# Last block's inverse by TensorE transposes, tokens stationary in the expert layer, rows of h on VectorE, a new order

## The chip, the cores and the metric

The kernel runs on one core of a Trainium2 chip, in one launch. The metric is device time in microseconds (us). Engines are called TensorE (PE), VectorE (DVE), ScalarE (ACT), GpSimd (POOL) and SyncE (SP, which issues nearly all transfers). Tensors on the chip lie on 128 partitions; TensorE writes to PSUM, and VectorE or ScalarE must copy results out of it.

## The reference, cut to what matters

Token count S is 2048, channels D are 640, inputs are bfloat16. Mixer A is a long convolution over tokens (an FFT of length 4096 in the reference), mixer B sends the 8 tokens with the largest router score through a gated expert layer and adds the result to their rows.

```python
def A(q, k, v, shift_k, ssm_k, ssm_D):
    kv = causal_conv4(k, shift_k) * v              # per channel, 4 taps
    y = irfft(rfft(kv, 2*S) * rfft(ssm_k, 2*S))[:S]  # per channel, over tokens
    return q * (y + kv * ssm_D)
def B(x, w_r, w_gate, w_up, w_down):
    r = x @ w_r; idx = argsort(-r)[:8]; xs = x[idx]
    y = (silu(xs @ w_gate) * (xs @ w_up)) @ w_down     # 640 -> 1728 -> 640
    return x.at[idx].add(y * sigmoid(r[idx]))
sa, ca, ga, sb, cb, gb = (silu(c) @ w_mod).reshape(6, 640)
x = A_q
x = x + ga * A(layernorm(x) * (1 + ca) + sa, A_k, A_v, ...)
x = x + gb * B(layernorm(x) * (1 + cb) + sb, ...)
```

Here h is layernorm(x)*(1+ca)+sa times ga, the factor on y; it is needed for every token and channel.

## The kernel before, in words

The 640 channels are five blocks of 128 (b = 0 to 4), the tokens 16 tiles of 128. A block goes through: G and X (first transform stage of the filter and of kv, line 435), BG and BX (second stage, 501, copied out into HX), P (the product in the frequency domain on VectorE, 513 to 519), BT (the first half of the inverse, 538, copied out of PSUM as U), UW and LU (U written to DRAM, 546, and read back in another layout as uA, 556: this exchanges channels with one of the token digits between partitions), AT (the second half, 575, which leaves tokens on the partition and is multiplied by h, 83 to 89), AA (added onto x, 586). Then R (594 on: transposes of x by TensorE, 644, copied out as xT, and the router's and the mean's dot products, 654) and GR (the squares of every row by small products, 596) run per block; when all five are summed, T makes the second layernorm's factors and picks the 8 tokens (860 to 901). The tail runs N (normalised rows, 839 and 842), BS and BL (x plus a row, 614 to 638), F (two VectorE passes over pairs of token tiles and the store to the output, 850 to 853), and between them the gather of the 8 rows (917), the gate and up products (935), the product hT (970) and the down product (978). The last step adds 40 pieces of 128 channels onto the output with an indirect transfer (988), after all stores have landed.

Lines 71 and 73 are the common copy out of PSUM: on VectorE where an entry of the order carries a star, else on ScalarE. t_H (line 787) makes h: a tensor_scalar for each of 16 token tiles (on GpSimd under a star), and two VectorE passes of 4 tiles by 640 (792).

The order is written out by hand: the string ORDER names task steps, and a loop runs them one after the other; each engine executes its own instructions in that order, and SP issues transfers one after the other, each behind the waits of those ahead. SLOTS gives the buffer of each allocation. In the functions below, tails of long helpers that the diff leaves alone are as in the program.

Of the kernel before, what the change touches and what calls it, by code (L numbers as in the profile page):

```python
# [22 lines left out]
NFC = 14  # L23
FFP = NFC * P
# [51 lines left out]
def _kernel_body(ctx, tc, A_q, A_k, A_v, A_shift_k, A_ssm_k, A_ssm_D,  # L76
# [75 lines left out]
    v_d = A_v.flatten_outer_dims().rearrange("(m p) d -> p m d", p=P)  # L152
    xq_d = A_q.flatten_outer_dims().rearrange("(m p) d -> p m d", p=P)
# [78 lines left out]
    keys = const.tile([P, M], F32, name="keys")  # L232
    mask8 = const.tile([NB * NSEL, NSEL], F32, name="mask8")
# [92 lines left out]
    def t_TC():  # L326
# [197 lines left out]
    def t_BT(b):  # L524
        hx = HXs[b]
        Ud = Uds[b] = dram.tile([P, M, 256], BF, name="Ud%d" % b)
        for hk in range(2):
            U = ring.tile([P, 8, 256], BF, name="U", tag="K", bufs=5)
            for kk in range(2):
# [10 lines left out]
                evac(U[:, 4 * kk:4 * kk + 4, :], ps[:])  # L540
                Us[b, hk] = U
# [24 lines left out]
    def t_AT(b):  # L566
        h = h_["h"]
        c0 = b * P
        for hb in range(2):
# [11 lines left out]
            yield  # L581

# [58 lines left out]
    def t_R(b):  # L641
        pt = ps_tile([P, M, P], BF)
        for m in range(M):
            nc.tensor.transpose(pt[:, m, :], xq[:, m, b * P:(b + 1) * P], ident[:])
        xTs[b] = ring.tile([P, M, P], BF, name="xT", tag="K", bufs=5)[:]
        if b == NB - 1:
            V.tensor_copy(out=xTs[b][:, 0:8, :], in_=pt[:, 0:8, :])
            nc.scalar.copy(out=xTs[b][:, 8:M, :], in_=pt[:, 8:M, :])
        else:
            evac(xTs[b], pt[:])  # L650
        yield
# [42 lines left out]
    def rows(i, scale, gate, shift):  # L694
# [4 lines left out]
        V.tensor_tensor(out=cg[:, NB:2 * NB], in0=modc[:, shift, :], in1=modc[:, gate, :], op=ALU.mult)  # L699
        pt = ps_tile([2 * NB, P], BF)  # L700
# [96 lines left out]
    def t_WG():  # L797

        w_sb = W["g"] = ring.tile([P, NB, FFP], BF, name="wg", tag="A", bufs=2)
        nc.gpsimd.memset(w_sb[:, :, FF:FFP], 0.0)  # L800
# [3 lines left out]
        w_sb = W["u"] = ring.tile([P, NB, FFP], BF, name="wu", tag="A", bufs=2)  # L804
        nc.gpsimd.memset(w_sb[:, :, FF:FFP], 0.0)
# [50 lines left out]
    def t_T():  # L856
# [220 lines left out]
```

## Time and profile before

| what | us |
|---|---|
| median of 3 runs | 178.72 (177.79 to 180.08) |
| profiled execution, its own time | 177.24 |
| its span, first to last instruction | 175.2 |
| VectorE busy / TensorE busy / ScalarE busy | 150.5 / 143.5 / 138.7 |

The median is 1.48 us above the profiled execution, and that 2.04 us above its span. A busy share over the whole span hides that the first 118 us and the last 57 us are bound differently; the rows below are therefore taken by stretch.

### The profile page before, as it was taken

The numbers are of one execution on the slowest core, as the hardware profiler recorded it, in microseconds if no ns is written. First come the engines' busy times: TensorE is split into PE (matmuls) and PEld (weight loads), VectorE is DVE, ScalarE is ACT, GpSimd is POOL, SyncE is SP. The second block draws the span as 40 slices with busy tenths as digits, with TensorE's granted clock in tenths as the row PEclk, the third lists the DMA queues.
The fourth block names the chain that finished last, engine by engine and source line by source line (L and its number), as shares of the span: only waits on it lengthen the run. The fifth ranks groups of instructions, "written<-read, shape, count | busy, mean of one in ns | idle before, by whom it ended". The sixth has DMA issues, their size and how long they took to land.

```text
span 175.2 us, 5348 instructions
## 1 busy us (share of the span) xinstructions
PE 143.5 (82%) x2296; PEld 118.2 (67%) x2299; DVE 150.5 (86%) x277; ACT 138.7 (79%) x156; POOL 57.1 (33%) x80
## 2 busy tenths in 40 slices
PE   7898997999899999889796999999679492699310
PEld 2487976887778867768685878988579440647300
DVE  7799999999999989999999999999946487799710
ACT  3769998999999999679987999999924249989200
POOL 8106299999000035909993001000000040000003
PEclk9999999999999999999999999999978879569655
DMA  6999999999995499478075782869792900495420
GB/s 135 207 230 226 260 269 259 207 282 322 283 310 122 99 321 247 172 199 280 23 223 239 205 261 120 281 207 308 230 343 34 332 13 2 105 340 185 146 77 2
DMA packets 54550, 35.51 MB, mean 203 GB/s; under 512 B 32057, under 2 KB 51966, under 8 KB 54526
## 3 DMA queue, kind: packets, MB, share of 16 engines
q1 hardware_dynamic: 54320, 35.15, 71.2%
q8 instruction: 18, 0.29, 0.8%
q0 software_dynamic: 80, 0.01, 0.2%
q14 instruction: 6, 0.05, 0.1%
q10 hardware_dynamic: 126, 0.01, 0.0%
HBM read 24.67 MB, written 7.87 MB: 186 GB/s over the span
## 4 chain that ended last, share of the span: by engine, by line
DVE 46%; PE 21%; DMA 13%; issue 7%; ACT 5%; POOL 3%; SPq 3%; POOLq 1%; DVEq 0%; ACTq 0%
DVE st L775 5%; DVE HX L514 5%; DVE T L513 5%; DMA Ud<-U 4%; DVE h L792 4%; DVE HX L71 4%; DVE kv L89 4%; DMA uA<-Ud 3%; PE ps L538 3%; DMA vN<-in_A_v_dram 3%; DMA out_dram<-IT 3%; SPq L163 2%; PE ps L473 2%; DVE A L71 2%; PE ps L435 2%
## 5 line engine op out<-in xcount | busy, mean ns | idle before, releaser
L73 ACT CAST A<-ps 128x1024 bf16<-128x1024 f32 x28 | 27.7, 1043 | 2.5 <-PE ps L435 2.5
L73 ACT CAST HX<-ps 128x1024 bf16<-128x1024 f32 x26 | 26.2, 1056 | 0.3
L787 POOL TENSOR_SCALAR h<-xq,rs,nm 128x640 bf16<-128x640 bf16 x12 | 19.9, 1671 | 2.1 <-PE p L435 2.1
L473 PEld LDWEIGHTS <-kT 128*128 128x128 bf16 x320 | 18.4, 98 | 3.0 <-issue 1.4
L501 PE MATMUL ps<-A,FX 128*128 128x256 bf16 x132 | 18.3, 273 | 1.8 <-DVE U L71 1.2
L538 PE MATMUL ps<-IT,HX 128*128 128x256 bf16 x112 | 18.0, 273 | 0.6 <-DVE HX L519 0.3
L501 PEld LDWEIGHTS <-FX 128*128 128x128 bf16 x160 | 14.7, 97 | 5.3 <-issue 3.3
L538 PEld LDWEIGHTS <-HX 128*128 128x128 bf16 x160 | 15.2, 98 | 3.4 <-issue 1.2
L73 ACT CAST U<-ps 128x1024 bf16<-128x1024 f32 x13 | 13.3, 1037 | 1.0 <-PE ps L538 0.7
L514 DVE TENSOR_TENSOR HX<-HX 128x2048 bf16<-128x2048 bf16 x10 | 13.7, 1374 | 0.3
L775 DVE BATCH_NORM_STATS2 st<-xq 128x6 f32<-128x320 bf16 x32 | 13.6, 478 | 0.0
L375 POOL TENSOR_SCALAR dg<-ident,shk_f 128x128 bf16<-128x128 bf16 x12 | 9.1, 772 | 13.0 <-DVE trig L408 8.8
L792 DVE TENSOR_TENSOR h<-h,modv 128x2560 bf16<-128x2560 bf16 x8 | 12.5, 1566 | 0.0
L575 PE MATMUL ps<-RAT,uA 128*128 128x128 bf16 x144 | 10.1, 232 | 2.9 <-DMA uA<-Ud 2.9
L73 ACT CAST base<-ps 128x1024 bf16<-128x1024 f32 x8 | 7.8, 1014 | 5.7 <-PE ps L620 5.7
L575 PEld LDWEIGHTS <-uA 128*128 128x128 bf16 x160 | 10.0, 104 | 3.3 <-DMA uA<-Ud 3.1
L513 DVE TENSOR_TENSOR T<-HX 128x2048 bf16<-128x2048 bf16 x10 | 12.1, 1214 | 0.0
L473 PE MATMUL p<-dg,kT 128*128 128x128 bf16 x160 | 10.1, 219 | 1.5 <-DVE dg L375 0.7
L538 PE MATMUL ps<-IT,T 128*128 128x256 bf16 x56 | 10.7, 273 | 0.0
L435 PEld LDWEIGHTS <-gF 128*64 128x64 bf16 x160 | 8.1, 109 | 3.7 <-issue 3.3
L988 POOL DMA_INDIRECT out_dram<-delta,idx x1 | 1.7, 1677 | 26.7 <-issue 26.7
L435 PEld LDWEIGHTS <-xA 128*64 128x64 bf16 x160 | 8.2, 109 | 3.2 <-issue 2.8
(263 smaller groups left out, 369.8 us busy)
## 6 DMA issues: line engine op xcount, KB each, us to landing
Ud<-U SPq DMA_DIRECT2D x10, 512.0 KB, 3.7
uA<-Ud SPq DMA_DIRECT2D x10, 512.0 KB, 5.3
early<-in_w_mod_dram SPq DMA_DIRECT2D x6, 800.0 KB, 7.6
gA<-in_A_ssm_k_dram SPq DMA_DIRECT2D x5, 512.0 KB, 6.6
vN<-in_A_v_dram SPq DMA_DIRECT2D x5, 512.0 KB, 5.5
xq<-in_A_q_dram SPq DMA_DIRECT2D x4, 640.0 KB, 6.4
wg<-in_B_w_gate_dram SPq DMA_DIRECT2D x5, 432.0 KB, 6.5
wu<-in_B_w_up_dram SPq DMA_DIRECT2D x5, 432.0 KB, 7.2
```

Source lines behind the costliest of these rows:

```text
L71: self.nc.vector.tensor_copy(out=out, in_=in_)
L73: self.nc.scalar.copy(out=out, in_=in_)
L435: nc.tensor.matmul(ps[o, bb // 2, :, (bb % 2) * 8:(bb % 2) * 8 + 8].rearrange("p (k c) e -> p k c e", c=2), lhsT=src[:, 4 * g4 + bb, o], r ...
L473: nc.tensor.matmul(ps[:, i, :], lhsT=kT[:, n0 - j:n0 - j + P], rhs=diags[b][:, j, :], start=(j == 0), stop=(j == 3))
L501: nc.tensor.matmul(ps[:, i], lhsT=FX[:, k2, :], rhs=A[:, 2 * k2:2 * k2 + 2, u, :], start=True, stop=True)
L513: V.tensor_tensor(out=T2[:], in0=X, in1=Hi, op=ALU.mult)
L514: V.tensor_tensor(out=X, in0=X, in1=Hr, op=ALU.mult)
L538: nc.tensor.matmul(ps[:, i, :], lhsT=a, rhs=IT[:, k2, d:d + 2, :].rearrange("p a b -> p (a b)"), start=(n == 0), stop=(n == len(terms) - 1))
L575: nc.tensor.matmul(o, lhsT=uA[:, bb, cs * P:(cs + 1) * P], rhs=RAT[:, cs, :].rearrange("p (m e) -> p m e", e=8), start=(cs == 0), stop=(cs ...
L775: V.bn_stats(out=st1[:, m, hf, :], in_=xq[:, m, hf * 320:hf * 320 + 320])
L787: (nc.gpsimd if evac.vector else V).tensor_scalar(out=h[:, m, :], in0=xq[:, m, :], scalar1=rs1[:, m:m + 1], scalar2=nm1[:, m:m + 1], op0=A ...
L792: V.tensor_tensor(out=hq, in0=hq, in1=row[:, None, :].to_broadcast([P, 4, D]), op=op)
```

## The change

The changed program does this. Block 4 no longer goes through DRAM: its BT copies are written in a strided layout, 16 blocks of 128x128 per half are transposed by TensorE (t_XT), copied out by VectorE and ScalarE, multiplied with the same table RAT with the data stationary, and give the inverse with channels on the partition. For that layout q's last block is read with a transposing transfer (t_LQT), h's last block is transposed by TensorE and scaled on the way out (t_HT), the sum is the xT that R and GR need, and t_RB transposes it back into x. In the expert layer the 8 tokens (padded to 32) are the stationary operand, in four column groups of 32 that take different tokens or columns; the gather's four partial sums are added by a product with S8. Hidden size 1728 is cut as 16 x 108, not 13.5 x 128. The rows of h are all on VectorE, and the two passes skip the last block. ORDER and SLOTS are new throughout; the strings are not shown beyond a line.

```diff
-UW4 AT1* AA0 BT4 LU3 BT4 AA0 AA1 AT2 LU3 GB:2 UW4 WG COL LU4 AA1 AT2* AA2:2 R0 AT3*:2 GR R1 LU4 AA3 R2 AA3 AT4 R0 GR
+BX4 AA1 P4 AT2* GR AA2 BG4 AA2 R1 BT4 UW3 P4 BT4 LU3 LQT GR P4 HT R2* AT3* R1 LU3 BT4 AA3 BT4 AT3 WG R2 AA3 XT BS* GR
 def t_BT(b):
-                evac(U[:, 4 * kk:4 * kk + 4, :], ps[:])
+                if b < NB - 1:
+                    evac(U[:, 4 * kk:4 * kk + 4, :], ps[:])
+                else:
+                    k0 = 8 * hk + 4 * kk
+                    for hf in range(2):
+                        o = Us[b][hf][:, :, :, k0:k0 + 4]
+                        i_ = ps[:].rearrange("p k (c j) -> p c j k", c=2)[:, :, 64 * hf:64 * hf + 64, :]
+                        ...
+def t_LQT():
+    lT["q"] = ring.tile([P, M, P], BF, name="qT4", tag="V")
+    nc.sync.dma_start_transpose(out=lT["q"][:]..., in_=q_d[:, (NB - 1) * P:D])
+def t_HT():
+    for m in range(M):
+        nc.tensor.transpose(pt[:, m, :], h_["h"][:, m, (NB - 1) * P:D], ident[:])
+    nc.scalar.activation(out=lT["h"][:], in_=pt[:], func=ACT.Identity, scale=hcol[:, 0:1], bias=hcol[:, 1:2])
+def t_XT():
+    for hf in range(2):
+        for i in range(M):
+            nc.tensor.transpose(pt[:, i, :], U[:, i * P:(i + 1) * P], ident[:])
+        V.tensor_copy(out=Vs[hf][:, 0:8, :], in_=pt[:, 0:8, :])
+        nc.scalar.copy(out=Vs[hf][:, 8:M, :], in_=pt[:, 8:M, :])
+    for hf in range(2):
+        for i in range(8):
+            for cs in range(2):
+                nc.tensor.matmul(ps[:, i, :], lhsT=Vs[hf][:, 8 * cs + i, :], rhs=RAT[:, cs, :], start=(cs == 0), stop=(cs == 1))
+        times(chunk(tT[:, :, hs]), ps[:]..., chunk(lT["h"][:, :, hs]))
+        V.tensor_tensor(out=xT[:, :, hs], in0=lT["q"][:, :, hs], in1=tT[:, :, hs], op=ALU.add)
 def t_H():
-                (nc.gpsimd if evac.vector else V).tensor_scalar(out=h[:, m, :], in0=xq[:, m, :], ...)
-            hq = h[:, 4 * m4:4 * m4 + 4, :]
+                V.tensor_scalar(out=h[:, m, :], in0=xq[:, m, :], ...)
+            hq = h[:, 4 * m4:4 * m4 + 4, 0:w]      # w = 512
 # gather, gate and up, down
-                nc.tensor.matmul(pxs[:, b, :] ..., lhsT=xq[:, m, b * P:(b + 1) * P], rhs=onehot[:, m, :], ...)
+                    nc.tensor.matmul(pX[32 * j:32 * j + 32, f0:f1], lhsT=oh32[:, m, :], rhs=xq[:, m, f0:f1], ...,
+                                     tile_position=(0, 32 * j))
+        V.tensor_copy(out=xg[:, 0:256], in_=pX[:, 0:256])
+        nc.scalar.copy(out=xg[:, 256:D], in_=pX[:, 256:D])
+            nc.tensor.matmul(px[:, NSEL * b:NSEL * b + NSEL], lhsT=xg[:, b * P:(b + 1) * P], rhs=S8[:], ...)
-                    nc.tensor.matmul(pp[:, fc - f0, :], lhsT=w_sb[:, b, fc * P:(fc + 1) * P], rhs=xsT[:, b, :], ...)
+                    nc.tensor.matmul(pp[32 * j:32 * j + 32, :], lhsT=xsT[:, b, :], rhs=w_sb[:, b, FQ * j:FQ * j + FQ], ...,
+                                     tile_position=(0, 32 * j))                       # FQ = 432
+        V.tensor_tensor(out=hh[:], in0=gs[:], in1=pgu[1][:], op=ALU.mult)
+            nc.tensor.transpose(pT[0:FC, i, :], hh[:, FC * i:FC * i + FC], ident[:])   # 4 of them
+        V.tensor_copy(out=hT[0:FC], in_=pT[0:FC]...)
+                for t in range(f0, f0 + 8):                                            # 80 products, 70 before
+                    nc.tensor.matmul(pyT[:, b, :], lhsT=W["d"][0:FC, t, b * P:(b + 1) * P], rhs=hT[0:FC, t % 4, t // 4, :], ...)
```

The order on the queues moves at three places that matter below. First SP, the transfers around the last round trip, before (Ud is the DRAM copy of U, the number tells blocks apart: 1889 is block 3, 2036 block 4; wu and wd are expert weights):

```order
L546 DMA Ud_1889<-U 128x2048
L546 DMA Ud_2036<-U 128x2048
L556 DMA uA<-Ud_1889 128x8x256 x2
L546 DMA Ud_2036<-U 128x2048
L807 DMA wu<-in_B_w_up_dram 128x1728
L556 DMA uA<-Ud_2036 128x8x256 x2
L807 DMA wu<-in_B_w_up_dram 128x1728 x3
```

and now (1846 is block 3, the last that goes through DRAM):

```order
L570 DMA Ud_1846<-U 128x2048 x2
L580 DMA uA<-Ud_1846 128x8x256
L609 DMA_TRANSPOSE qT_2353<-in_A_q_dram 128x2048
L580 DMA uA<-Ud_1846 128x8x256
L881 DMA wg<-in_B_w_gate_dram 128x1728 x2
L885 DMA wu<-in_B_w_up_dram 128x1728 x2
```

Block 4's four transfers are gone, and the transposing read of q stands between the two halves of block 3's read.

Second VectorE, from the last product P of block 4 (519) on, before:

```order
L519 TENSOR_TENSOR HX<-HX,T_2010 128x8x128
L87 TENSOR_TENSOR t<-t,h 128x1024 x4
L586 TENSOR_TENSOR xq<-xq,t 128x16x64 x3
L89 TENSOR_TENSOR t<-ps,h 128x1024
L719 TENSOR_SCALAR mc<-modc 128x5
```

and now (527 is the same product, 561 the copy of block 4's last U):

```order
L527 TENSOR_TENSOR HX<-HX,T_2337 128x8x128
L71 COPY xT<-ps 128x2048
L87 TENSOR_TENSOR t<-t,h 128x1024
L734 TENSOR_TENSOR rsum<-rsum,pq 128x48
L665 TENSOR_TENSOR xq<-xq,t 128x16x64
L561 CAST U<-ps 128x128x4
L89 TENSOR_TENSOR t<-ps,h 128x1024
L734 TENSOR_TENSOR rsum<-rsum,pq 128x48
L665 TENSOR_TENSOR xq<-xq,t 128x16x64
L634 COPY V<-ps 128x1024
```

The multiplications and additions of blocks 0 to 2 (and xT copies) now stand ahead of block 4's last U, not behind it.

Third VectorE at the very end, before:

```order
L850 TENSOR_TENSOR IT<-IT,modv 128x1280
L970 TENSOR_TENSOR hT<-gs,ps 128x56 x2
L852 TENSOR_TENSOR IT<-IT,base 128x1280
L981 COPY yT<-pg 128x40
L986 SCALAR_TENSOR_TENSOR delta<-pq,sig,gb_119 40x128
```

and now:

```order
L1041 TENSOR_TENSOR gs<-gs,pg 128x432
L1046 COPY hT<-ps 108x128
L928 TENSOR_TENSOR IT<-IT,base 128x1280
L926 TENSOR_TENSOR IT<-IT,modv 128x1280
L928 TENSOR_TENSOR IT<-IT,base 128x1280
L926 TENSOR_TENSOR IT<-IT,modv 128x1280
L1056 COPY yT<-pg 128x40
L928 TENSOR_TENSOR IT<-IT,base 128x1280
L1061 SCALAR_TENSOR_TENSOR delta<-pq,sig,gb_119 40x128
```

The copy of the down product's result (yT) now stands ahead of the last add of F (928).

## Rows read from the trace of the kernel before

**Rows 1.** Page: span, and each engine's busy time with its share.
```profile
span 175.2 us, 5348 instructions
PE 143.5 (82%) x2296; PEld 118.2 (67%) x2299; DVE 150.5 (86%) x277; ACT 138.7 (79%) x156; POOL 57.1 (33%) x80
```

**Rows 2.** Stretches: length; busy PE, PEld, DVE, ACT, POOL; granted clock, DMA share, GB/s.
```profile
0.00:118.40 118.40, 108.56 (x1405) 90.32 (x1406) 113.45 (x180) 106.20 (x120) 53.14 (x71) 1.00 0.83 222
118.40:142.10 23.70, 18.03 (x574) 16.45 (x573) 16.35 (x39) 12.37 (x10) 1.41 (x6) 0.87 0.72 232
145.40:165.50 20.10, 11.96 (x263) 8.76 (x265) 17.43 (x42) 17.25 (x24) 0.00 (x0) 0.77 0.49 166
165.50:175.20 9.70, 1.73 (x51) 1.35 (x48) 0.57 (x3) 0.00 (x0) 1.68 (x1) 0.50 0.16 44
...
164.80:167.50 2.70, 2.39 (x71) 2.05 (x71) 0.93 (x2) 0.00 (x0) 0.00 (x0) 0.50 0.68 238
```

**Rows 3.** Chain of waits (start, us, what): block 4's round trip, and the end.
```profile
118.42 4.07 DMA Ud<-U
122.57 5.62 DMA uA<-Ud
...
165.56 4.50 DMA out_dram<-IT
```

**Rows 4.** Timeline of VectorE and GpSimd (start, us): h, with and without GpSimd beside it.
```profile
69.69 1.78 DVE L514 TENSOR_TENSOR HX<-HX 128x2048 bf16<-128x2048 bf16 x1
71.40 3.04 DVE L787 TENSOR_SCALAR h<-xq,rs,nm 128x640 bf16<-128x640 bf16 x4
78.82 14.73 POOL L787 TENSOR_SCALAR h<-xq,rs,nm 128x640 bf16<-128x640 bf16 x8
93.00 1.62 DVE L514 TENSOR_TENSOR HX<-HX 128x2048 bf16<-128x2048 bf16 x1
...
104.03 1.23 DVE L514 TENSOR_TENSOR HX<-HX 128x2048 bf16<-128x2048 bf16 x1
145.41 0.45 DVE L839 TENSOR_SCALAR xn<-xq,sn 128x640 bf16<-128x640 bf16 x1
```

**Rows 5.** Groups by line: xcount | busy us, mean ns of one | idle before.
```profile
L792 DVE TENSOR_TENSOR h<-h,modv 128x2560 bf16<-128x2560 bf16 x8 | 12.5, 1566 | 0.0
L586 DVE TENSOR_TENSOR xq<-xq,t 128x1024 bf16<-128x1024 bf16 x10 | 6.5, 686 | 0.0
L89 DVE TENSOR_TENSOR t<-ps,h 128x1024 bf16<-128x1024 f32 x3 | 3.7, 1223 | 3.9 <-PE ps L575 3.9
L647 DVE COPY xT<-ps 128x1024 bf16<-128x1024 bf16 x1 | 0.7, 691 | 0.4 <-PE ps L644 0.4
L648 ACT COPY xT<-ps 128x1024 bf16<-128x1024 bf16 x1 | 1.0, 1013 | 1.2 <-DVE xT L647 1.2
```

**Rows 6.** Timeline of TensorE matmuls (start, us to the end of the last).
```profile
118.74 1.07 PE L575 MATMUL ps<-RAT,uA 128*128 128x128 bf16 x16
128.24 1.31 PE L575 MATMUL ps<-RAT,uA 128*128 128x128 bf16 x16 [2.90 <-DMA uA<-Ud]
129.89 0.70 PE L596 MATMUL pg<-xT 128*32 128x32 bf16 x64
130.52 1.89 PE L575 MATMUL ps<-RAT,uA 128*128 128x128 bf16 x16
164.82 2.01 PE L978 MATMUL pg<-hT,wd 128*128 128x8 bf16 x70 [3.01 <-DVE hT L970]
```

**Rows 7.** Timeline of SP's queue (start, us that the issue held it).
```profile
31.23 0.52 SPq L167 DMA_DIRECT2D vN<-in_A_v_dram  x1
59.37 8.13 SPq L163 DMA_TRANSPOSE kT<-in_A_k_dram  x1
```

**Rows 8.** Timeline of VectorE in the tail, with the idle time before a row.
```profile
152.54 0.20 DVE L922 TENSOR_TENSOR xa<-pq,mc 128x40 f32<-128x40 f32 x1 [1.11 <-PE pq L917]
160.24 0.83 DVE L852 TENSOR_TENSOR IT<-IT,base 128x1280 bf16<-128x1280 bf16 x1
```

More of the change, by code (lines that the diff above doesn't have):

```diff
@@ L583, in t_AA, with t_RB @@
+    def t_RB():
+        for hf in range(2):
+            ms = slice(8 * hf, 8 * hf + 8)
+            pt = ps_tile([P, 8, P], BF)
+            for i in range(8):
+                nc.tensor.transpose(pt[:, i, :], xTs[NB - 1][:, 8 * hf + i, :], ident[:])
+            evac(xq[:, ms, (NB - 1) * P:D], pt[:])
+            yield
+    lT = {}
     def t_AA(b):
@@ L641, in t_R @@
     def t_R(b):
[L642 to L649, printed above, removed]
+        if b < NB - 1:
+            pt = ps_tile([P, M, P], BF)
+            for m in range(M):
+                nc.tensor.transpose(pt[:, m, :], xq[:, m, b * P:(b + 1) * P], ident[:])
+            xTs[b] = ring.tile([P, M, P], BF, name="xT", tag="K", bufs=5)[:]
             evac(xTs[b], pt[:])
-        yield
+            yield
         pr = small_ps([P, M, 3])
@@ L699, in rows @@
         V.tensor_tensor(out=cg[:, NB:2 * NB], in0=modc[:, shift, :], in1=modc[:, gate, :], op=ALU.mult)
+        if i == 0:
+            for a in range(2):
+                V.tensor_copy(out=hcol[:, a:a + 1], in_=cg[:, NB * a + NB - 1:NB * a + NB])
         pt = ps_tile([2 * NB, P], BF)
@@ L899, in t_T @@
         V.max(out=t8[:], in_=cand.bitcast(F32))
-        onehot = tail()[:, 1280:1408].rearrange("p (m s) -> p m s", m=M)
+        onehot = oh32[:, :, 0:NSEL]
         V.tensor_tensor(out=onehot, in0=keys[:, :, None].to_broadcast([P, M, NSEL]),
@@ L928, in t_T @@
-        V.tensor_tensor(out=xsT[:, 3:5, :], in0=xsf[:, 3:5, :], in1=xb[:, 3:5, :], op=ALU.add)
+        V.tensor_tensor(out=xsf[:], in0=px[:, 0:NB * NSEL].rearrange("p (b s) -> p b s", b=NB), in1=xa[:], op=ALU.mult)
+        V.tensor_tensor(out=xsT[:, :, 0:NSEL], in0=xsf[:], in1=xb[:], op=ALU.add)
         yield
-        def proj(pp, w_sb, f0, f1):
+        pgu = small_ps([P, FQ]), other_ps([P, FQ])
+        gs = small.tile([P, FQ], BF, name="gs")
+        for pp, w_sb in zip(pgu, (W["g"], W["u"])):
@@ L945, in t_T @@
-        for i in range(2):
-            proj(pup[:, i, 0:HF * NSEL].rearrange("p (f s) -> p f s", s=NSEL), W["u"], i * HF, i * HF + HF)
+                for j in range(4):
+                    nc.tensor.matmul(pp[32 * j:32 * j + 32, :], lhsT=xsT[:, b, :], rhs=w_sb[:, b, FQ * j:FQ * j + FQ],
+                                     start=(b == 0), stop=(b == NB - 1), tile_position=(0, 32 * j), skip_group_check=True)
+        nc.scalar.activation(out=gs[:], in_=pgu[0][:], func=ACT.Silu)
         yield
```

157 lines of the change are left out of this document (91 added, 66 removed).

## The prediction, made before the changed kernel was run

> **What bounds the kernel now.** I read the page first: VectorE is busy longest, but at 86% [rows 1], so the share has to be split. The stretches do that [rows 2]. Up to 118.4 us VectorE works 113.45 us, TensorE has its full clock, and whatever VectorE is given there lengthens the stretch. From 118.4 to 142.1 VectorE works only 16.35 of 23.70 us and ScalarE 12.37: nobody is full, so something else sets the end. The chain of waits says what [rows 3]: after block 4's last copy the data goes to DRAM (118.42) and back (122.57), and TensorE starts the second half of its inverse at 128.24 [rows 6], 9.8 us later. Everything behind it (R, GR, the second layernorm) waits for that block. From 145.4 to 165.5 VectorE is near its limit again, 17.43 of 20.10 us, with F's sixteen passes as the body. The last 9.7 us are the last store (4.50 us), the scatter and its landing, and contain almost no work.
>
> So the end is a sum of four: t0 (block 4's last U copy, 118.4), 23.7 to the start of T, 3.3 for T, 20.1 for the tail, 9.7. Durations on VectorE I count from start to start, 0.07 to 0.09 below a row's length (the product of 69.69 lasts 1.78, the next operation starts at 71.40 [rows 4]; F's pass is 0.83 long [rows 8] and counts 0.75).
>
> **Up to t0: what VectorE is given and spared.** Idle time there I leave as it is, 5.0 us.
> - Rows of h: twelve go from GpSimd to VectorE. The four already there took 3.04 us, 0.76 each, while GpSimd ran the same operation; the same shape and operation took 0.45 alone (145.41) [rows 4]. 12 x 0.42 = +5.0. With the crowded price it would be 9.1.
> - The two passes over h are 512 instead of 640 wide: 8 x 1.566 / 5 = -2.5 [rows 5].
> - Crowding ends: between 69.69 and 93.00 twelve VectorE operations that read SBUF ran longer than the same form elsewhere, the product of 2048 elements 1.78 and 1.62 against 1.23 [rows 4]. The excesses add up to 4.9 us, and no row of h is left on GpSimd: -4.9.
> - Moved ahead of t0 from behind it: three products with PSUM (1.13), six additions (0.60), two copies xT of 2048 elements (twice L647's 0.69, less overlap, 1.3), some eighteen small ones (1.9 in all) [rows 5]: 3.4 + 3.6 + 2.6 + 1.9 = +11.5. This work was in the half-empty stretch; it now sits in the full one, and that is the price of the change.
> - Copies out of PSUM given to ScalarE: four of HX less, three of A more, U's a half instead of a whole, one of modv and half a kv product less, net -3.0. Small things (diagonals to GpSimd, one negation from it): +0.5.
>
> Together +6.6, t0 = 125.0. ScalarE takes the extra copies and half of the moved xT, TensorE about 9 us of moved products; both had 10 to 12 us free in the 118.4 [rows 2], and the new stretch is 6.6 longer.
>
> **From t0 to T.** Before t0, AT of blocks 0 to 2, their R and two of five GR are done. Behind it VectorE has 9.8 us of work, and the chain runs: the last product and addition of block 3 and the copy V (1.1 + 0.6 + 0.7, with TensorE's 16 transposes beside them; ScalarE's half 1.0 [rows 5]), ready at t0 + 3.1. Sixteen products 1.07 [rows 6], 4.2; R's transposes of block 3 and the second sixteen, 6.2; product and addition with q 1.8, 8.0. Then R's small products (0.5), GR (0.70 [rows 6]), two passes over the squares (half L89's length each) and small ones: t0 + 10.9. T starts at 135.9, 6.2 earlier. The strided copies of U and the product with a strided h have no row; the same element counts bound them from below, twice that (0.6 more for each of four that wait) from above; I take the former since kv's products permute too and cost no more than plain ones.
>
> **The transposing read.** A transposing issue holds SP 8.13 us at worst, a plain one 0.52 [rows 7]. Behind q's stands the second half of block 3's read. Block 3's U is copied some 19 us before t0 (an estimate: ScalarE's copies in between, about 1 us each, as L648 [rows 5]), its write lands 4 later, the issue ends at t0 - 7 at worst, and the read needs 5.6 [rows 3]: t0 - 1, just in time for its products at t0. I count nothing, with no cover to spare. [...]
>
> **The tail.** VectorE gets an addition of 1024 elements (0.6), two normalised rows that ScalarE had (0.85), the gather's copy (0.35), a wider product and copy for hT (0.6 more), loses two small operations (-0.35): about +2.0 with rounding. ScalarE loses as much, so it does not bind. The wait of 1.11 us at the gather [rows 8] stays at 0 to 1.5: 80 small products go, 16 groups of four streams of 512 or 128 columns come, then two copies and five products. Two waits are new: hT (transposes in between, 0.5) and yT, where the last F pass now stands behind the down products. Those are 80 small ones; 70 took 2.01 at granted clock 0.50 [rows 2, 6], so the low clock doesn't hurt them: 2.3, with four streams of 512 columns ahead, against four F passes (3.0) as cover, 0.4 to 1.2 left. The tail had 2.7 us of idle time [rows 2]; I let old and new waits cancel: +2.0, between +0.5 and +4.5.
>
> Gate and up are 40 streams of 432 columns in four column groups. No row shows that; with four side by side (64 products of 32 columns took 0.70, 11 ns each [rows 6], less than one such column run) it is 10 x 0.2 = 2.0, one after another 8. I take 2.0, and 3.6 at the low clock, against 140 small products, 3.8 to 4.0 at the price above. [...]
>
> **Sum.** 175.2 - 6.2 + 2.0 = 171.0 for the span, 173.0 with the 2.04 us around it, against 177.24 for the profiled execution. The median of the runs stands 1.48 higher, so 174.5.
>
> **Rivals.**
> [...]
> 2. *Better filled.* VectorE's 5.0 us of idle time before t0 falls to 3 and the tail costs +0.5: span 167.5, median 171.
> 3. *The moved products wait in front of block 4 (slower).* TensorE executes in order, and AT of blocks 1 to 3 now stands ahead of block 4's BT. Where their uA has not landed, all of block 4 waits, as it did 9.8 us for its own before. One such wait of 2.9 us for each of three blocks (the wait before 128.24 [rows 6]) makes t0 133.7: span 179.7, median 183.2. Below one such wait it decides nothing; it takes two to lose the gain. Against: the writes are issued well ahead in the new queue. For: one SP queue carries them, and q's transposing read and the weights are in it.
> 4. *The round trip wasn't what held the end*, since VectorE is the bound anyway and only its order changed: then only the balance counts, +2.0 in the tail, -2.4 of spared work: within 2%.
>
> **Chances.** The forecast 0.40, rival 2 0.11, rival 1 with 4 0.31, rival 3 0.18. A measurement of this kernel tells about 2% from no change (175.1 to 182.3). The forecast is just beyond that edge, and a part of it, about 0.06, falls inside, as some of rival 1 falls short of it: faster 0.50, same 0.33, slower 0.17. The range reaches from rival 2 to the near end of rival 3: 170.5 to 181.5; the likeliest case alone is 172.5 to 176.5 by its unknown waits.
>
> **What would show it.** Right: no write or read of block 4; the last U copy near 125 and T near 136; rows of h at 0.4 to 0.5 each and the product of 2048 elements at 1.23 throughout; gate and up in 2 to 4 us; the last F pass 20 to 24 us behind T's end. Wrong: h's rows still at 0.8; TensorE waiting for uA ahead of block 4's BT; a granted clock of 0.5 between t0 and T; a VectorE wait of over 2 us at yT or at the gather. If t0 is beyond 129, the step on filling VectorE failed; if T is more than 12.5 behind t0, the step on the new chain.

## The result, and the profile after

| | median us (runs) | ratio to the kernel before, 95% interval |
|---|---|---|
| before, with one run more than above | 178.29 (177.79 to 180.08) | |
| changed | 172.37 (170.36 to 172.72) | 0.9627, 0.9525 to 0.9729 |

3.7% faster. The forecast was 174.5 with a range of 170.5 to 181.5. The profiled execution took 172.72 with a span of 170.9; the sum had said 173.0 and 171.0. That it is so close is luck: the tail came out 1.3 us longer than in the sum, t0 and the stage behind it together 1.1 longer, the end 2.3 and T 0.2 shorter. The two largest, tail and end, both come from the way in which TensorE's instructions arrive; most of this text is about them. Executions fall into two states, of which the ratios compare the faster one alone, while the medians and the profiled executions of a_trip, a_hpool and b_pad include the slower.

The page of the changed kernel, its head and the instruction queue of TensorE, to be read beside [rows 1]:

```profile
span 170.9 us, 5177 instructions
PE 143.9 (84%) x2214; PEld 114.7 (67%) x2214; DVE 151.5 (89%) x293; ACT 137.7 (81%) x157; POOL 38.6 (23%) x71
q8 instruction: 17, 0.28, 0.7%
```

Stretches, columns as in [rows 2]: up to block 4's last copy of U (t0), on to the start of T (to 137.0), the tail, the end.

```profile
0.00:125.60 125.60, 119.33 (x1693) 98.56 (x1693) 119.57 (x217) 113.17 (x128) 35.75 (x65) 1.00 0.87 220
125.60:137.00 11.40, 8.44 (x325) 7.75 (x322) 10.02 (x18) 4.47 (x4) 0.98 (x4) 1.00 0.73 193
140.10:163.50 23.40, 16.17 (x203) 8.39 (x202) 19.14 (x46) 20.03 (x25) 0.00 (x0) 0.79 0.36 126
163.50:170.90 7.40, 0.00 (x0) 0.00 (x0) 0.27 (x2) 0.00 (x0) 1.68 (x1) 0.50 0.16 46
```

So t0 is 125.6 (118.4 before), the new stage 11.4 (23.7), T 3.1 (3.3), the tail 23.4 (20.1), the end 7.4 (9.7). VectorE's timeline: four rows of h, the last copy of U, the first step of T (its last, 959, ends at 140.06), and what comes behind it.

```profile
79.02 1.51 DVE L867 TENSOR_SCALAR h<-xq,rs,nm 128x640 bf16<-128x640 bf16 x4
124.98 0.68 DVE L561 CAST U<-ps 128x512 bf16<-128x512 f32 x1
136.95 0.17 DVE L936 SCALAR_TENSOR_TENSOR n2v<-ssq,msq 128x16 f32<-128x16 f32 x1
142.89 0.69 DVE L708 TENSOR_TENSOR base<-xq,modv 128x1024 bf16<-128x1024 bf16 x1 [2.83 <-ACT xq L73]
```

Right behind T VectorE waits 2.83 us for a copy of ScalarE, and ScalarE waits 8.73 us, until 141.84, for TensorE. TensorE's timeline says why; the two rows at 152.12 and 153.05 are the gate and up products in their new form.

```profile
133.17 0.55 PE L730 MATMUL pq<-wcol,xT 128*128 128x3 bf16 x16 [1.12 <-ACT xT L73]
133.65 0.66 PE L675 MATMUL pg<-xT 128*32 128x32 bf16 x64
134.28 0.54 PE L730 MATMUL pq<-wcol,xT 128*128 128x3 bf16 x16
134.75 0.66 PE L675 MATMUL pg<-xT 128*32 128x32 bf16 x64
135.35 0.56 PE L656 MATMUL ps<-ident,xT 128*128 128x128 bf16 x7
141.54 0.27 PE L656 MATMUL ps<-ident,xT 128*128 128x128 bf16 x1 [5.63 <-issue]
...
152.12 1.10 PE L1017 MATMUL pq<-wg,xsT 128*32 128x432 bf16 x20 [0.64 <-DVE xsT L1008]
153.05 1.09 PE L1017 MATMUL pg<-wu,xsT 128*32 128x432 bf16 x20
```

TensorE stops for 5.63 us after seven of eight equal transposes, whose operands are all there. "issue" means that it waited for nothing that the profile knows. The DMA view offers a candidate: queue q8, of kind "instruction". Its 17 packets are 0.28 MB, 16 KB each, and of all engines only TensorE has instructions enough for them: 4,428 products and weight loads are some 260 per packet, 63 bytes each (the kernel before: 18 packets for 4,595, so 255 and 64 bytes). I read such a packet as a page of TensorE's own instructions. The view of 129.98 to 138.92, then of 138.9 to 140.1 (queue: packets, MB, share of 16 engines; q14 is another queue of instructions, with packets of half the size):

```profile
q1 hardware_dynamic: 1543, 2.28, 92.5%
q14 instruction: 1, 0.01, 0.2%
...
q8 instruction: 1, 0.02, 5.7%
```

For nine us no page arrives on q8, with the transfer engines 92.5% busy on weights (wd, 2.2 MB, was issued at 126.85 and 128.18, one of wu's transfers behind each); then one page comes, and TensorE goes on 1.5 us behind it. Ahead of the stop 167 products with as many weight loads ran in 2.7 us (133.17 to 135.9). That is more than one page, where on average a page lasts some 9 us (17 pages in 160 us).

The last store, in the chain of waits, against the last line of [rows 3]; and the transposing read of q on SP's queue:

```profile
163.58 2.28 DMA out_dram<-IT
```

```profile
109.75 5.19 SPq L609 DMA_TRANSPOSE qT<-in_A_q_dram  x1
```

### The profile page after: what moved, and what is told of

It reads as the page before. It is cut to its first block, busy times and chain, and to the rows that moved or that the text cites. A ratio compares the mean times of both kernels' runs of the same rounds, so it can differ in the third digit from the quotient of the medians.

```text
span 170.9 us, 5177 instructions
## 1 busy us (share of the span) xinstructions
PE 143.9 (84%) x2214; PEld 114.7 (67%) x2214; DVE 151.5 (89%) x293; ACT 137.7 (81%) x157; POOL 38.6 (23%) x71
## 4 chain that ended last, share of the span: by engine, by line
DVE 47%; PE 31%; issue 10%; ACT 8%; DMA 1%; POOLq 1%; ACTq 0%; DVEq 0%; SPq 0%
PE ps L550 6%; DVE kv L89 4%; DVE A L71 4%; DVE T L521 4%; DVE h L872 3%; PE ps L509 3%; PE ps L328 3%; PE ps L443 3%; DVE h L867 3%; PE ps L481 2%; DVE st L854 2%; ACT xT L73 2%; DVE HX L522 2%; PE p L550 2%; PE p L481 2%
## 5 line engine op out<-in xcount | busy, mean ns | idle before, releaser
L73 ACT CAST HX<-ps 128x1024 bf16<-128x1024 f32 x30 | 30.1, 1046 | 0.8 <-PE ps L509 0.7
L550 PE MATMUL ps<-IT,HX 128*128 128x256 bf16 x128 | 20.9, 273 | 0.2
L73 ACT CAST U<-ps 128x1024 bf16<-128x1024 f32 (+1 forms) x18 | 15.6, 906 | 1.8 <-PE ps L550 0.9
L383 POOL TENSOR_SCALAR dg<-ident,shk_f 128x128 bf16<-128x128 bf16 x16 | 14.2, 901 | 7.2 <-PE ps L481 4.3
L550 PE MATMUL ps<-IT,T 128*128 128x256 bf16 x72 | 13.7, 273 | 0.0
L481 PE MATMUL ps<-dg,kT 128*128 128x128 bf16 x192 | 12.0, 219 | 1.1 <-DVE dg L383 0.8
L443 PE MATMUL ps<-RA,gF 128*64 128x256 bf16 x136 | 10.0, 276 | 0.3 <-ACT A L73 0.3
L550 PEld LDWEIGHTS <-T 128*128 128x128 bf16 x96 | 9.4, 98 | 1.1
L872 DVE TENSOR_TENSOR h<-h,modv 128x2048 bf16<-128x2048 bf16 x8 | 9.8, 1219 | 0.2
L443 PE MATMUL ps<-RX,xA 128*64 128x256 bf16 x120 | 9.0, 277 | 0.3 <-ACT xA L73 0.3
```

The lines of the kernel that those rows point to most:

```text
L73: self.nc.scalar.copy(out=out, in_=in_)
L383: (nc.gpsimd if evac.vector else V).tensor_scalar(out=dg[:, j, :], in0=ident[:], scalar1=shk_f[:, b, j:j + 1], scalar2=None, op0=ALU.mult)
L443: nc.tensor.matmul(ps[o, bb // 2, :, (bb % 2) * 8:(bb % 2) * 8 + 8].rearrange("p (k c) e -> p k c e", c=2), lhsT=src[:, 4 * g4 + bb, o], r ...
L481: nc.tensor.matmul(ps[:, i, :], lhsT=kT[:, n0 - j:n0 - j + P], rhs=diags[b][:, j, :], start=(j == 0), stop=(j == 3))
L550: nc.tensor.matmul(ps[:, i, :], lhsT=a, rhs=IT[:, k2, d:d + 2, :].rearrange("p a b -> p (a b)"), start=(n == 0), stop=(n == len(terms) - 1))
L872: V.tensor_tensor(out=hq, in0=hq, in1=row[:, None, 0:w].to_broadcast([P, 4, w]), op=op)
```

## The experiments

Kernels whose names begin with a are edits of the changed kernel, with b of the kernel before. Each was timed beside the kernel before (medians 178.7 to 179.0).

| run | median us (runs) | ratio to before, 95% interval |
|---|---|---|
| a_shift | 173.75 (173.67 to 174.28) | 0.9777, 0.9688 to 0.9866 |
| a_wdlate | 170.81 (170.32 to 171.56) | 0.9616, 0.9522 to 0.9710 |
| a_hpool | 174.34 (171.66 to 175.68) | 0.9707, 0.9555 to 0.9859 |
| a_oldexp | 172.26 (171.15 to 172.50) | 0.9666, 0.9567 to 0.9764 |
| after2 | 172.73 (170.59 to 173.65) | 0.9659, 0.9587 to 0.9731 |
| a_wdlate2 | 171.00 (170.62 to 171.99) | 0.9604, 0.9557 to 0.9652 |
| a_trip | 180.81 (178.33 to 182.99) | 1.0073, 1.0015 to 1.0131 |
| b_hV | 178.57 (176.56 to 182.13) | none given |
| b_pad | 177.29 (174.18 to 177.54) | none given |
| b_wdlate | 176.27 (175.48 to 177.42) | 0.9908, 0.9862 to 0.9954 |
| b_both | 175.60 (173.61 to 175.81) | 0.9863, 0.9785 to 0.9941 |
| a_padend | 171.65 (170.62 to 172.19) | 0.9651, 0.9563 to 0.9739 |

### What TensorE waited for: a_shift, a_wdlate

```diff
 def t_WU():                                   # a_shift
-        for i in range(13):
-            nc.tensor.matmul(pw[:], lhsT=z[:, 0:P], rhs=z, start=True, stop=True)
+        for i in range(120):
+            nc.tensor.matmul(pw[:, 0:56], lhsT=z[:, 0:P], rhs=z[:, 0:56], start=True, stop=True)
```

> The changed kernel with one edit: the warm-up at the start is 120 products of 56 columns in place of 13 of 512, nearly the same number of columns and 214 more TensorE instructions (each product has a weight load). Everything behind it is as it was. Theory 1, instruction supply: TensorE stood still for 5.63 us in the middle of eight transposes because the next 16 KB of its own instructions (256 of 64 bytes) had not arrived; the one packet of its instruction queue came at 138.93 to 140.02 and it went on at 141.54. With the boundaries of these pages 214 instructions further along, the page is asked for before the dense small products and the next one is not needed before about 146: the gap in the transposes falls below 0.5 us, VectorE's wait of 2.83 us at base goes, and the time falls by 2 to 3 us, to about 170 us, less up to 1 us if the longer warm-up holds the start. Theory 2, a dependency at this place of the program that the profile doesn't show (a buffer, or the small operations of the second layernorm): the gap stays where it is, 5 to 6 us, and the time stays at 172.4 or is up to 1 us more.

TensorE's timeline of a_shift, its start and the transposes back:

```profile
8.93 3.23 PE L481 MATMUL ps<-dg,kT 128*128 128x128 bf16 x32 [2.61 <-DMA kT<-in_A_k_dram]
...
138.00 1.04 PE L656 MATMUL ps<-ident,xT 128*128 128x128 bf16 x8
```

The stop is gone and VectorE's wait at base with it, though program and transfers are the same there: the place of the page boundaries moved (one page comes between 133.0 and 134.3, the next between 134.3 and 142.5), and the whole stage comes 2.7 us later. The dependency theory falls. The time did not fall by the 2 to 3 us that I expected, it rose to 173.75, for two reasons. The edit cost more at the start than the 1 us that I had allowed: the first products with kT began at 8.93, waiting for it, not at 7.63, took 1.0 us longer, and the last copy of U was 2.4 us late. And from base to the last store's issue 21.76 us went by, 20.69 in the changed kernel, at a granted clock of 0.61 from 142 to 150 and 0.70 from 156 to 162 against 0.75 and 0.81 (1.00 in both between), with waits of 0.76 us at hT (0.52) and 0.53 at yT (none).

```diff
 def t_WD():                                   # a_wdlate
-            nc.sync.dma_start(out=wd[0:FC, 8 * i:8 * i + 8, :], ...)
+            nc.scalar.dma_start(out=wd[0:FC, 8 * i:8 * i + 8, :], ...)
-... R4 GR:2 WG RB T BL* WG WD N N* T N:2 WG WD RB ...
+... R4 GR:2 WG RB WD:2 T BL* WG N N* T N:2 WG RB ...
```

> The changed kernel with one edit: the two transfers of wd (2.2 MB together) are issued by ScalarE behind its first copy of the transposes back, not by SyncE at 126.85 and 128.18. Instructions of TensorE are the same. Theory 1, instruction supply held up behind the weights: TensorE's page is asked for at about 133.8 in both, but without wd's 2.2 MB in the queues it arrives within 1 to 3 us, so the gap of 5.63 us falls to at most 2 us, VectorE's wait of 2.83 us at base falls below 1 us, and the time falls by 2 to 2.8 us to about 170 us. Theory 1b, the page is late for another reason than the traffic (it is simply 5 us from asking to landing): the gap stays above 4 us and the time at 172.4. The price of the edit: wd is issued near 138 and needs about 9 us at the 235 GB/s of that stretch, so it is there by 147 to 150, ahead of the down products at 159.6; nothing is expected from that.

The DMA view of a_wdlate from 129.4 to 135.0, then from 135.0 to 136.1; and TensorE's and VectorE's timelines:

```profile
DMA packets 0, 0.00 MB, mean 0 GB/s; under 512 B 0, under 2 KB 0, under 8 KB 0
...
q8 instruction: 1, 0.02, 5.3%
```

```profile
137.40 0.27 PE L656 MATMUL ps<-ident,xT 128*128 128x128 bf16 x1 [1.51 <-issue]
```

```profile
139.89 0.68 DVE L708 TENSOR_TENSOR base<-xq,modv 128x1024 bf16<-128x1024 bf16 x1
```

With no weights in the queues the same page comes 3.9 us earlier, the stop is 1.5 us and VectorE no longer waits. (SP no longer stands at wd, so wu's two transfers went out ahead as well: the edit takes these out of the stretch too, not wd alone.) Both edits agree: TensorE ran out of instructions, because a page came late during the weights' transfers. When a page is asked for no view shows; in a_wdlate this one moves from 135.06 on, so it was asked for by then; the 133.8 of the expectation was my estimate. It was worth 1.6 us of median where I expected 2 to 2.8. The repeat beside the changed kernel:

> The changed kernel again, unedited, beside the next one on the same chip: 172.4 us, ratio 0.96 to 0.97 by every theory. The gap of TensorE in the transposes back should be there again, 4 to 6 us long, ending 1.3 to 1.5 us behind the landing of the instruction packet.

> The version in which ScalarE issues wd's two transfers behind the first copy of the transposes back, again with five rounds, as the candidate for a version that beats both kernels. Instruction supply held up behind the weights: 1.5 to 2.8 us below the changed kernel run beside it, so about 170.5 us. If the first comparison was an accident of the run: within 0.5 us of it.

172.73 against 171.00, 1.7 us. Over ten runs each the medians are 172.55 and 170.99; the two intervals against the kernel before still overlap. The medians with late wd are the lowest of this study.

### The round trip alone: a_trip

```diff
 def t_XT():
+            if hf == 0:      # trip: pairs (U of a half, a DRAM tile of its size)
+                for Ux, Ud in trip:
+                    nc.sync.dma_start(out=Ud[:], in_=Ux)
+                for Ux, Ud in trip:
+                    nc.sync.dma_start(out=Ux, in_=Ud[:])
```

> The changed kernel with the DRAM round trip put back for block 4's data and nothing else: both halves of U are written to DRAM and read back into the same place before they are transposed. The prediction's step, that the trip held the end: T starts 9 to 10 us later (4.07 and 5.62 us for the two transfers in the kernel before), nothing stands ready to fill the gap, and the time rises by as much, to 181 to 183 us. Rival 4 of the prediction, the trip was not what held the end because VectorE is the bound anyway: the time rises by 2 us at most, to 174.5 us.

The chain of waits of a_trip, and TensorE's first transposes behind it:

```profile
126.19 3.32 DMA Ux<-U
129.53 6.01 DMA U<-Ux
```

```profile
132.23 1.86 PE L639 MATMUL ps<-ident,U 128*128 128x128 bf16 x16 [6.41 <-DMA U<-Ux]
```

The copy that is read back has plain rows here, not the old pieces. T starts at 145.78, 8.8 us later (in an execution 1.3 us above the median), and by the ratios of a_trip and after2, of one session, the time rises by 4.1% of the kernel before, 7.4 us. That is somewhat less than the 9 to 10 that I expected; still the trip held the end, little filled it, and rival 4 falls. The ratio to the kernel before is 1.0073: with the trip put back nothing of the gain is left. As a_trip also keeps the transposes and copies that take the trip's place, it does not say what the other parts of the change would gain with the old inverse.

### Rows of h: a_hpool and b_hV

```diff
 def t_H():                                    # a_hpool
-            for m in range(4 * m4, 4 * m4 + 4):
-                V.tensor_scalar(out=h[:, m, :], ...)
+            for m in (range(0, 8) if m4 == 0 else range(4 * m4 + 4, min(16, 4 * m4 + 8))):
+                (V if m < 4 else nc.gpsimd).tensor_scalar(out=h[:, m, :], ...)
-BT3 BX4* BX4 H* BG4 ...                       # b_hV: three such stars in ORDER
+BT3 BX4* BX4 H BG4 ...
```

> The changed kernel with one edit: twelve of the sixteen rows of h go back to GpSimd, each group of four one step ahead of the passes that read it, so that VectorE need not wait. The prediction's own step: VectorE saves 12 x 0.42 = 5.0 us and pays 4.9 us again in operations that run longer beside GpSimd, so the last U copy of block 4 stays within 1 us of 125.0 and the time within 1.5 us of 172.4. Rival A, crowding is small (the rows that were long in the kernel before were long for another reason): VectorE keeps its shapes' plain durations (product of 2048 elements 1.23 us), t0 is 4 to 5 us earlier, 168 us. Rival B, crowding is larger than the saving, or VectorE and TensorE wait for the slow rows (1.84 us each on GpSimd in the kernel before): t0 over 2 us later, 175 us or more.

> The kernel before with one part of the change alone: all sixteen rows of h on VectorE (the twelve of GpSimd too), in the old order and with passes of 640. By the prediction's step the two terms cancel (+5.0 us for the rows, -4.9 us for crowding): last U copy of block 4 within 1 us of 118.4, time within 1.5 us of 178.7. By what the reverse edit in the changed kernel showed (VectorE's busy time the same, 2.8 us more of waiting with GpSimd on the rows): 1 to 3 us faster, 176 to 177.5 us, with less idle time on VectorE ahead of block 4's last copy. Rival: the old order has the rows where ScalarE and TensorE need VectorE soon, so that 5 us more of work there delay t0: 181 us or more.

Timeline of a_hpool with GpSimd on the rows, and its stretch up to t0:

```profile
78.90 2.48 DVE L867 TENSOR_SCALAR h<-xq,rs,nm 128x640 bf16<-128x640 bf16 x4
79.04 21.67 POOL L867 TENSOR_SCALAR h<-xq,rs,nm 128x640 bf16<-128x640 bf16 x11 [0.43 <-PE ps L509]
90.54 1.78 DVE L522 TENSOR_TENSOR HX<-HX 128x2048 bf16<-128x2048 bf16 x1
```

```profile
0.00:128.90 128.90, 119.92 (x1695) 99.31 (x1696) 120.09 (x205) 113.39 (x128) 58.59 (x77) 0.99 0.83 215
```

And of b_hV, where VectorE does them all in the old order:

```profile
71.97 1.51 DVE L787 TENSOR_SCALAR h<-xq,rs,nm 128x640 bf16<-128x640 bf16 x4
```

```profile
0.00:119.90 119.90, 108.99 (x1405) 89.94 (x1406) 113.67 (x192) 106.62 (x120) 31.66 (x59) 1.00 0.85 219
```

VectorE's busy time up to t0 is 113.67 us with sixteen rows and 113.45 with four [rows 2]; the other way round, 120.09 with four against 119.57 with sixteen. The twelve rows and the crowding beside GpSimd weigh the same within some half a us, in both directions. VectorE's idle time ahead of t0 does not follow: 6.2 us in b_hV against 5.0 in the kernel before, 8.8 in a_hpool against 6.0 in the changed kernel. So t0 is 1.5 us later in b_hV's profiled execution: my expectation of t0 within 1 us missed there, and so did that of less idle time. In a_hpool's it is 3.3 us later, but that is the slowest of its four executions and says nothing sure of the others. In time neither is told from its kernel: b_hV's four runs reach from 176.56 to 182.13, which leaves my 1 to 3 us less open, and a_hpool's interval contains the changed kernel's ratio.

### The expert layer's form: a_oldexp

```diff
-        onehot = oh32[:, :, 0:NSEL]           # pX, xg, S8, four column groups of 432, 16 x 108
+        onehot = tail()[:, 1280:1408]...      # gather, gate, up, hT, down, WG and WD as in the kernel before
```

> The changed kernel with the expert layer in its old form: gather by 80 small products, gate and up with the weights stationary and 8 columns moving (140 products), hidden size in 14 pieces of 128, 70 down products; the order of the steps is that of the change. By the prediction's terms the new form costs VectorE 0.6 us (the gather's copy 0.35, hT 0.6, two small ones -0.35) and TensorE's products lie beside F's passes in both forms: the time stays within 1 us of 172.4. Rival: the tail is short because the products are: the old gather takes about 2.2 us (80 x 27 ns) against 1.3, gate and up 3.9 against 2.0, and as VectorE waits for both, the last F pass comes 2 to 3 us later, 175 us.

TensorE's gate and up products in a_oldexp, the first and the last (between them 35 more, for gate):

```profile
151.18 1.12 PE L1014 MATMUL pq<-xsT,wg 128*128 128x8 bf16 x35
153.09 2.01 PE L1014 MATMUL ps<-xsT,wu 128*128 128x8 bf16 x70
```

3.9 us against 2.0, as the two sums had it, and the same median within 0.1 us. But the two profiled executions did not have the same stop ahead of it: 3.83 us in a_oldexp and 5.63 in the changed kernel. VectorE's first row behind the stop, ScalarE's and VectorE's longest waits in the tail, and the last store of a_oldexp:

```profile
141.23 0.69 DVE L706 TENSOR_TENSOR base<-xq,modv 128x1024 bf16<-128x1024 bf16 x1 [0.89 <-ACT xq L75]
156.86 1.01 ACT L75 CAST base<-ps 128x1024 bf16<-128x1024 f32 x1 [1.42 <-PE ps L697]
159.53 0.83 DVE L928 TENSOR_TENSOR IT<-IT,modv 128x1280 bf16<-128x1280 bf16 x1 [2.26 <-ACT IT L920]
```

```profile
162.97 2.28 DMA out_dram<-IT
```

From base to the last store's issue a_oldexp takes 21.74 us, the changed kernel 20.69 (142.89 to 163.58). In the old form VectorE waits 2.26 us for ScalarE, which waits for the products of BS that stand on TensorE behind gate and up, at a granted clock of 0.50 from 150 to 158 (1.00 in the changed kernel). Against that only the new form has the waits at hT and yT's copy, 0.52 and 0.35. So the old form's products did not lie wholly under F's passes; its price of about 1 us is hidden in the medians by the shorter stop. Five other executions with the new form took 20.7 to 21.1 us, those of a_trip and a_shift 21.4 and 21.8, so that 1 us is not clear of the spread: the new form was worth some 1 us or less, and that it was worth nothing is not shown.

### The end, and the same supply in the kernel before: b_pad, b_wdlate, b_both, a_padend

Why does the last store land after 2.28 us, not 4.50? The DMA view of the kernel before from 166.6 to 170.2, in 40 slices of 0.09 us (busy tenths, GB/s):

```profile
DMA  9899899950000000000011001010000000000000
GB/s 384 313 523 370 313 370 341 327 171 14 0 0 0 0 0 0 0 0 0 0 14 14 0 14 14 0 28 14 28 28 14 28 28 0 0 0 0 0 0 0
...
q8 instruction: 1, 0.02, 2.7%
```

The store's data has moved by 167.4, but for a rest of 14 to 28 GB/s from 168.4 to 169.6. That rest is 17 packets of 0.02 MB together, about a sixteenth of the store's 320 KB, so I read it as the share of one of the 16 engines. One page of TensorE's instructions lies in this window; it took 2.7% of 16 engines for 3.6 us, which is 1.56 us of one engine. The changed kernel, 163.5 to 165.9 (slices of 0.06 us), has no page there and no rest:

```profile
DMA  0000000000000000599999999999998410000000
```

```diff
+        pad = other_ps([P, NSEL])             # b_pad, b_both: ahead of hT
+        for i in range(70):
+            nc.tensor.matmul(pad[:], lhsT=ident[:], rhs=ident[:, 0:NSEL], start=True, stop=True)
 def t_WD():                                   # b_wdlate, b_both: all three transfers
-        nc.sync.dma_start(out=wd[:, 0:7, :], ...)
+        nc.scalar.dma_start(out=wd[:, 0:7, :], ...)
-AA4 ... R2 TC R4 WG R3 COL ... T N WD N WG ... N BS WD N
+AA4 ... R2 TC R4 WD:2 WG R3 COL ... T N N WG ... N BS N
```

> The kernel before with 70 tiny products of 8 columns more (140 instructions, their result is read by nobody) ahead of the down products, where TensorE waits 3.0 us anyway. Theory, instruction supply at the end: in the kernel before, one transfer engine fetched TensorE's last page of instructions (16 KB) from 166.85 to 168.42, just as the last store's data moved, so this engine's share of the store moved from 168.40 on and the store landed 4.50 us after its issue, not 2.28 as in the changed kernel. With 140 instructions more the page is fetched near 163 to 165, the last store lands in 2.3 to 2.6 us, the end is 7.5 us instead of 9.7, and the time falls by 2 us, to 176.5 to 177 us. Rival: the store is slow because of its own traffic with the stores ahead of it (64% of the transfer engines busy between 164.8 and 167.5): it stays at 4.0 to 4.5 us, and the time at 178.7 or up to 0.5 us more.

> The kernel before with wd's three transfers issued by ScalarE behind block 4's last copy xT, where it is idle for 5 us, not by SyncE at 133.73 and 150. Instructions of TensorE are the same. In the kernel before TensorE stood still for 2.25 us (to 139.23) in the squares' small products, with its page of instructions arriving at 136.05 to 137.77. Theory, instruction supply held up behind the weights: the page comes near 135.2 to 136.2, the gap falls to at most 1 us, T starts 1 to 1.5 us earlier, and the time falls by as much, to 177.3 to 177.8 us. Rival, the page's own latency: the gap stays at 2 us or more, the time at 178.7. Price of the edit: three issues on ScalarE, 0.4 us each, in its idle time.

> The kernel before with both edits, the wd transfers late and the 70 tiny products, beside the kernel before. If both costs are of TensorE's instruction supply, they add: 3 to 3.7 us below the kernel before, about 175.2 us, ratio 0.98. Then the distance to the version of the changed kernel with late wd transfers (170.9 us), 4.3 us, is what the change's own steps are worth, and the rest of the measured 6.2 us between the two kernels came from where the pages of instructions fall. If they don't add, or aren't there, the ratio is above 0.99.

> The changed kernel with 36 tiny products of 8 columns more (72 instructions, read by nobody) ahead of hT's transposes, where TensorE waits 3.4 us anyway: the reverse of the edit at the end of the kernel before. A page of instructions more is then needed, and asked for near the end of the down products (162.0 to 162.5), if my count of the instructions is right to about 10. Theory, instruction supply at the end: the page moves between 163.3 and 165, together with the last store, one transfer engine's share of it is late, the store lands in 3.3 to 4.5 us instead of 2.28, and the time rises by 1 to 2.2 us, to 173.5 to 174.8 us. If the count is off, the trace shows no page there, and the time stays at 172.5. Rival, traffic of the stores alone: a page there, and the store still lands in 2.3 us.

The last store in the chain of waits of b_pad, then b_wdlate, then b_both:

```profile
167.57 2.77 DMA out_dram<-IT
```

```profile
164.63 4.06 DMA out_dram<-IT
```

```profile
166.28 2.28 DMA out_dram<-IT
```

Where a page falls on the last store (the kernel before, b_wdlate, and b_hV with 3.88) it lands in 3.9 to 4.5 us; where the page comes ahead of it (b_both) or none is near (the changed kernel and a_padend) in 2.3. The other edits of the changed kernel land at 2.28 too, without a view of their pages. B_pad's store took 2.77: no page starts between 167.5 and 170.4, and a rest of 18 to 35 GB/s lies ahead of its data and behind it. That fits a page just ahead of 167.5, later than I had counted, but no view shows it. B_pad's time, 177.29 without a ratio, does not tell whether the 2 us that I expected are there, as a longer stop (3.48 us, 2.25 in the kernel before) stands on its way to T. The rival of the stores' own traffic falls: the stores are the same.

The kernel before had stops of the same kind; one on the way to T, from TensorE's timeline, then the same products in b_wdlate:

```profile
139.23 0.25 PE L596 MATMUL pg<-xT 128*32 128x32 bf16 x8 [2.25 <-issue]
```

```profile
137.79 0.59 PE L596 MATMUL pg<-xT 128*32 128x32 bf16 x56
138.85 0.23 PE L596 MATMUL pg<-xT 128*32 128x32 bf16 x8 [0.46 <-issue]
```

B_wdlate gains 1.6 us by its ratio (0.9908), about as expected, and the stop is 0.46 us. The way is not quite the one expected: in the profiled execution T starts 0.45 us earlier (141.69 against 142.14), not 1 to 1.5, since the products behind the round trip began 0.9 us later. B_both gains 2.4 us by its ratio (0.9863), short of the 3 to 3.7 that I expected; in its profile a stop of 2.43 us stands at another place, 132.87, and T starts at 142.20, as in the kernel before, so what it gains there is at the end. That the two costs add is not shown. A_padend had no page at the end (none on q8 from 157.2 to 170.4, so my count of instructions was off) and no change of time; it tells only that its 36 products in TensorE's idle time cost nothing measurable.

## Why the prediction came out right, and where it didn't

- **Up to t0**: 125.0 said, 125.6 measured. VectorE's busy time 113.45 + 6.6 = 120.05 against 119.57; the idle time rose to 6.0 where I had left 5.0. Rows of h at 1.51 for four (0.38 each), the product of 2048 elements at 1.23 throughout, both as written. That the rows and the crowding cancel was the least certain term, and in busy time two edits confirm it. Both were sized half a us too large: twelve rows at 0.38 are 4.5, not 5.0, and with the 0.22 by which b_hV's busy time is above the kernel before's the crowding is 4.3, not 4.9.
- **t0 to T**: 10.9 said, 11.4 measured, with waits of VectorE (0.95) for the products with data stationary and of TensorE (1.12) for ScalarE's copy xT. The trip's price is shown by a_trip.
- **The transposing read** held SP 5.19 us, less than the 8.13 allowed; block 3's second read was issued at its end and no product waited for it.
- **Gate and up**: 2.0 said, 2.0 measured, at a granted clock of 1.00 (152.1 to 154.1). In the kernel before one product of 512 columns started every 0.21 us at that clock (156.41 to 157.06). By an estimate from it 432 columns take 0.18 and forty one after another 7.1 us: the four column groups ran 3.6 times as fast. No run shows them at the low clock, for which I had taken 3.6 us.
- **The tail**: the failed step is "I let old and new waits cancel: +2.0". It is +3.3, inside my bounds, and 2.83 of it is one wait that the prediction did not look for: TensorE without instructions. Without it the tail would be 20.6, +0.5, the lower bound that I gave; in a_wdlate, where VectorE has no such wait, it is 21.0. HT's wait of 0.52 came as said and the gather's fell to nothing; at yT VectorE did not wait for the products, 0.35 us of idle time stand behind its copy. That gate and up lie beside F's passes held for the new form; for the old one a_oldexp shows a wait of 2.26 us.
- **The end**: the sum leaves its 9.7 us as they were, and that failed too: it is 7.4. 2.2 us of the 9.7 were the page that held up the last store; the changed kernel's last page comes at another time.
- **The median**: I added 1.48 us for the distance of the profiled execution to the median before. After, the median lies 0.35 below the profiled one. That is most of the 2.1 us between 174.5 and 172.4.
- **Clock and rivals**: a granted clock of 0.5 between t0 and T, a sign against the prediction, did not show: it was 1.00 there and fell during the stop, to 0.72 from 137 to 142. Rival 3 did not happen: no wait for uA ahead of block 4's BT. 4 fell with a_trip. The version with late wd comes near 2 in its span (168.4 for 167.5), but not by its mechanism: VectorE's idle time before t0 is 5.9 us there, not 3.

Seen whole, with a part of both kernels' supply costs taken out, the ratios of b_both and a_wdlate2 (0.9863 and 0.9604) are 4.6 us apart, where the two kernels as they are were 6.1 to 6.7 apart (0.9659 and 0.9627). The 4.6 for the change itself is an estimate: the sessions differ, the intervals leave it some 1.6 us either way, a stop of 2.43 us remains in b_both, and one of 1.51 us stands in a_wdlate, the same edit as a_wdlate2.

## What to carry to other kernels

When a chain ends in "issue" on TensorE, count its instructions: here a stage of 167 small products used more than a page of them in 2.7 us, and with a large load in the queues the next page came late. Start bulk loads ahead of or behind such a stage, not in it: late wd was worth 1.6 to 1.7 us here. Before an engine's work is made shorter, see whether anyone waits for it: the expert layer's products were halved for some 1 us or less, while putting the DRAM trip back cost 7.4, as much as the whole gain. And before two equal medians are read as "no effect", look whether something else differs between them, as the stop does between a_oldexp and the changed kernel.

## What the hardware showed that I had not expected

- TensorE's instructions share the transfer engines with the data: the pages of 16 KB shown above took 0.9 to 1.6 us each. One came behind weights, with a stop of 5.63 us (1.5 with empty queues). One moved beside a store's data and left about a sixteenth of the store for 168.4 to 169.6; the kernel before's last store landed at 4.50, where stores without a page landed at 2.28. From a page's landing to the next product 1.4 to 1.5 us went by in a_wdlate, the kernel before and the changed kernel.
- The granted clock behind the stop does not simply follow it: from 142 to 150 it was 0.75 in the changed kernel and 0.97 in a_wdlate, but 0.61 in a_shift, which has no stop there, and 0.93 in a_oldexp, whose stop is 3.83 us. In the changed kernel no VectorE wait hung on it: behind base its longest are 0.52 at hT and 0.35 behind yT, both after 156.
